# Bringing x in transposed by DMA instead of transposing it on TensorE

## The chip, the cores and the metric

The kernel runs on one core of a Trainium2 chip. The metric is the device time of one execution in microseconds. A core has TensorE (PE in the profile, with weight loads as PEld), VectorE (DVE), ScalarE (ACT), GpSimd (POOL) and SyncE (SP); SP, ACT and POOL also have queues that issue DMAs.

## The reference

One input x of 2048 rows and 448 channels goes through two branches that a gate mixes: attention with 16 query heads of 28 channels over one shared key and value head, and a state-space convolution along the rows.

```python
x = A_x                                              # (1, 2048, 448) bf16
g = _sigmoid((x * gate_w).sum(-1, keepdims=True))
q = (x @ wq).reshape(B, S, H, Dh) ...                # H = 16, Dh = 28
k = x @ wk;  v = x @ wv
scores = einsum("bhqd,bkd->bhqk", q, k) * (Dh ** -0.5)
a = (softmax(scores) @ v) ... @ wo
P = exp(dt * (A_re + 1j*A_im) * l)                   # 448 channels, 256 modes, l = 0..2047
K = einsum("dn,dnl,dn->dl", Cc, P, dB).real          # a kernel of 2048 taps for each channel
b = causal_convolution(K, x) + x * Dskip             # the reference does it by FFT
return g * a + (1 - g) * b
```

## The kernel before, in words

The kernel is written as a list of operations with their data dependences (`Prog.op`, `Prog.dma`). A planner (`Prog.schedule`) gives each operation an estimated duration, a priority `pr` and, where `pg.after[i] = d` is set, a predecessor it has to follow in the plan without waiting for it on the chip; it writes down one fixed order for each engine. `Prog.emit` then puts a semaphore wait where an operation depends on another engine or a DMA. Every DMA is issued on line 140 by the queue that `eng` names, so one line stands for all of them in the profile, and they are told apart by their tiles. An instruction that waits holds back everything behind it on its engine or queue.

**Start.** The K, V and q projections contract over channels, so x is needed with channels on partitions. `loads` brings x in as it lies (four chunks `x0` to `x3` of 512 rows into the tile `tab`), and `prep_x` transposes each chunk: 16 transposing matmuls (L613) into PSUM and two copies to SBUF, on ACT (L623) or DVE (L625). A transposed chunk holds four blocks `T` of 112 channels in 512 columns each, where block T takes channels 4p + T. Chunk 0 lies in `xT`, chunk 1 in a free part of `T`, chunks 2 and 3 in slots of `expT` that are not yet used. The weights are brought in the same channel order (`wks` in `seedw`, `wst` in `mbf`) and spread by DVE copies into `Wk` (L526), `Wq` (L528) and `Wv` (L530, L532).

For each chunk, four matmuls make K (L633), ACT copies it to `kT` (L645), DVE takes the largest absolute value of each row (L640), and 16 small matmuls make V and the gate's argument (L656). When all four chunks are through, DVE takes the largest of the four values (`kap`, L665) and makes `Wb` from it (L667). `qproj` makes q for a group of four heads over 512 rows: four matmuls with `Wq` (L810), a reduction on DVE (L816), one matmul with `Wb` (L819) that adds a bound on each score as one more channel, and a cast to `qT` (L822). So no score can be made before all of K.

**Scores.** 1024 tiles of 128 keys by 512 queries, in sets of two or three: the scores on PE (L1186, or L1209 from a spread copy `qM` of q), one exponential on ACT for the whole set (L1230), and the sums with V on PE (L1248). q is made two groups ahead. A chunk of queries serves four groups; then its successor is brought into `xT`. Chunks 1 to 3 were stored for this in a DRAM scratch `XS` (three stores from SP during the start), and `qproj` reloads them on POOL's queue.

**Convolution.** In the same time `prep_params` transposes six raw parameter arrays on PE (`raw0` to `raw5`, L738) and multiplies them out on DVE (L749); `masters` and `tables` build powers of the modes on DVE (L867 to L937), `kgen` makes the taps on PE, POOL stores them to a DRAM scratch `KP`, SP brings them back as banded tiles (`tload`, into `T` and later `U`), and `conv` multiplies these with a shifted copy `U` of x. `U` is zeroed by one DMA, and x comes once more into `O` by sixteen DMAs, from which POOL copies it into `U` and `T`. These DMAs are planned behind the scratch stores of the transposed x (`self.late`).

Of the kernel before, what the change touches and what calls it, by code (L numbers as in the profile page):

```python
# [12 lines left out]
P = 128  # L13
# [66 lines left out]
class Prog:  # L80
# [55 lines left out]
    def dma(self, pairs, desc, slot, rd=(), wr=(), pr=0, eng="sp", slow=False, extra=0):  # L136
        kw = dict(allow_slow_non_contiguous=True) if slow else {}
# [243 lines left out]
class Kernel:  # L381
# [26 lines left out]
    def alloc(self):  # L408
# [44 lines left out]
        self.XS = nc.dram_tensor("XS_scratch", (3 * DT * XQ,), BF).ap()  # L453
# [40 lines left out]
    def loads(self):  # L494
        pg, ins = self.pg, self.ins
        self.xst = self.tab
        x = ins["A_x"]

        def lx(q):
            pg.dma([(self.xst.v(0, P, q * 4 * D, [[1, 4 * D]]), dram(x, q * 4 * P * D, [[4 * D, P], [1, 4 * D]]))],  # L500
                   (128, 3584), f"x{q}", wr=[("xst", q)])
# [5 lines left out]
        def lraw(k):  # L507
            pg.dma([(raw.v(0, DT, k * 1024, [[1, 1024]]), dram(ins[names[k]], 0, [[1024, DT], [1, 1024]]))],
                   (112, 2048), f"raw{k}", wr=[("raw", k)])
# [3 lines left out]
        lx(0)  # L513
        pg.dma([(wks.v(0, DT, 0, [[1, 112]]), dram(ins["A_wk"], 0, [[112, DT], [1, 112]])),
                (wks.v(0, DT, 112, [[1, 112]]), dram(ins["A_wv"], 0, [[112, DT], [1, 112]])),
                (wks.v(0, DT, 224, [[1, 4]]), dram(ins["gate_w"], 0, [[4, DT], [1, 4]]))],
               (336, 200), "wk", wr=["wks"], eng="act")
        lx(1)
        pg.dma([(wst.v(0, DT, 0, [[1, 4 * D]]), dram(ins["A_wq"], 0, [[4 * D, DT], [1, 4 * D]]))],
               (112, 3584), "wq", wr=["wqs"], eng="act")  # L520
        pg.dma([(self.dtb.v(0, P, 0, [[1, D]]), dram(ins["B_log_dt"], 0, [[0, P], [1, D]]))], (128, 896), "ldt", wr=["dt"], eng="act")
        lraw(0)
        lx(2)
        lx(3)
        lraw(1)
        pg.op("dve", lambda e: e.tensor_copy(self.Wk.v(0, DT, 0, [[32, 16], [1, DH]]),  # L526
                                             wks.v(0, DT, 0, [[DH, 4], [0, 4], [1, DH]])), 300, rd=["wks"], wr=["Wk"])
        pg.op("dve", lambda e: e.tensor_copy(self.Wq.v(0, DT, 0, [[32, 64], [1, DH]]),  # L528
# [71 lines left out]

    def prep_x(self):
        pg = self.pg
        xst, kT = self.xst, self.kT
        sm = self.small
        for q in range(4):
            for hp in range(2):
# [733 lines left out]
```

## Time and profile before

| | |
|---|---|
| median of 3 runs | 516.68 us (514.37 to 519.31) |
| the profiled execution | 515.85 us, span 514.0 us |
| busy: ACT / DVE / PE / POOL | 484.5 / 456.7 / 436.6 / 164.1 us |
| exponentials on ACT, L1230 | 465.8 us in 410 instructions |
| first exponential | at 24.0 us |
| DMA queue of SP and that of ACT | 80.76 MB and 0.57 MB |

The span is that of the profiled execution, from its first to its last instruction; the time has what lies around it too. Busy shares are averages over the span; which engine sets the pace is read for each stage.

### The profile page before, as it was taken

The page shows a single profiled execution, that of the slowest core. Times are in us where ns is not written, and L with a number is a line of the kernel's source. Part 1 is how long each engine was busy: PE and PEld are TensorE (multiplying, and loading weights), DVE is VectorE, ACT ScalarE, POOL GpSimd, SP SyncE. Part 2 cuts the span into 40 slices and gives each one's busy share as a digit, 9 for nine tenths or more (in the row PEclk, how much of TensorE's full clock was granted, in tenths as well). Part 3 has the DMA queues.
Part 4 walks back from the last instruction along what each step waited for, and adds up shares of the span by engine and source line. Part 5 has one row for each costly group of instructions (what it writes and reads, how often), then busy time and mean ns, then how long its engine had stood idle before and what let it go on. Part 6 is the DMA issues. An engine that isn't in the chain of part 4 may idle for free.

```text
span 514.0 us, 16906 instructions
## 1 busy us (share of the span) xinstructions
PE 436.6 (85%) x7376; PEld 199.3 (39%) x7468; DVE 456.7 (89%) x856; ACT 484.5 (94%) x434; POOL 164.1 (32%) x306
## 2 busy tenths in 40 slices
PE   5777968789898999889787889989888889989887
PEld 4532113244442434344343433444333444445542
DVE  3899999999999999999999999999999999972223
ACT  3898899999999999999999999999999999999992
POOL 5103624215123425034305242612313162324110
PEclk9969588999997999999999999999999999999997
DMA  8996189945709484985946767794953766097911
GB/s 256 258 246 166 12 174 110 301 119 153 240 8 279 131 261 59 255 192 157 238 112 192 159 199 179 188 269 117 287 125 117 256 200 215 13 321 227 297 31 36
DMA packets 151603, 91.93 MB, mean 179 GB/s; under 512 B 83469, under 2 KB 147518, under 8 KB 151530
## 3 DMA queue, kind: packets, MB, share of 16 engines
q1 hardware_dynamic: 141978, 80.76, 58.6%
q0 software_dynamic: 8896, 9.53, 7.4%
q8 instruction: 58, 0.95, 0.8%
q10 hardware_dynamic: 656, 0.57, 0.4%
q14 instruction: 15, 0.12, 0.1%
HBM read 73.71 MB, written 5.23 MB: 154 GB/s over the span
## 4 chain that ended last, share of the span: by engine, by line
ACT 77%; PE 11%; DVE 6%; DMA 4%; issue 1%; SPq 1%; ACTq 0%; DVEq 0%; another core or an unknown queue 0%
ACT expT L1230 77%; DMA T<-KP_scratch 3%; PE psS L1209 2%; PE psS L1186 1%; PE psB L1248 1%; DMA seedw<-in_gate_w_dram 1%; PE psX L1020 1%; PE psS L1130 1%; SPq L140 1%; DVE tab L749 1%; PE psS L633 1%; PE psS L810 1%; PE psS L613 0%; PE psS L1020 0%; PE psX L810 0%
## 5 line engine op out<-in xcount | busy, mean ns | idle before, releaser
L1230 ACT ACTIVATE expT<-psS 128x1536 bf16<-128x1536 f32 (+1 forms) x410 | 465.8, 1370 | 9.3 <-PE psS L1186 3.7
L901 DVE TENSOR_TENSOR tab<-tab,mbf 128x512 bf16<-128x512 bf16 (+4 forms) x140 | 139.8, 1001 | 0.0
L1209 PE MATMUL psS<-qM,kT 128*128 128x512 bf16 x301 | 101.8, 399 | 26.9 <-ACT expT L1230 14.2
L1186 PE MATMUL psS<-qT,kT 29*128 29x512 bf16 x570 | 77.4, 398 | 27.0 <-ACT expT L1230 25.1
L1248 PE MATMUL psB<-expT,vaug 128*32 128x512 bf16 x960 | 98.5, 402 | 0.2
L140 POOL DMA_DIRECT2D KP_scratch<-kstg x112 | 61.4, 555 | 109.4 <-DVE kstg L970 96.7
L916 DVE TENSOR_TENSOR tab<-tab 128x256 bf16<-128x256 bf16 (+4 forms) x140 | 77.4, 576 | 0.0
L140 POOL DMA_DIRECT2D qM<-qT x64 | 32.5, 516 | 75.0 <-DVE qT L822 63.0
L1248 PEld LDWEIGHTS psB<-expT,vaug 128*32 128x32 bf16 x960 | 24.6, 93 | 76.4 <-issue 73.4
L140 POOL DMA_DIRECT2D rdenB<-R_scratch x60 | 30.1, 509 | 50.6 <-DMA R_scratch<-denT 50.6
L1186 PEld LDWEIGHTS psS<-qT,kT 29*128 29x128 bf16 x570 | 18.7, 91 | 67.9 <-ACT expT L1230 58.4
L1209 PEld LDWEIGHTS psS<-qM,kT 128*128 128x128 bf16 x390 | 23.9, 99 | 47.6 <-ACT expT L1230 33.9
L1020 PE MATMUL psS<-T,U 128*26 128x128 bf16 (+3 forms) x1728 | 38.9, 221 | 1.3 <-issue 1.0
L1020 PE MATMUL psX<-T,U 128*26 128x128 bf16 (+3 forms) x1536 | 35.4, 223 | 2.2 <-DMA T<-KP_scratch 2.2
L1020 PEld LDWEIGHTS psS<-T,U 128*26 128x26 bf16 (+3 forms) x1728 | 29.9, 105 | 16.0 <-issue 11.6
L1020 PEld LDWEIGHTS psX<-T,U 128*26 128x26 bf16 (+3 forms) x1536 | 27.1, 106 | 15.9 <-issue 9.1
L930 DVE TENSOR_TENSOR tab<-tab,tmp 128x1984 bf16<-128x1984 bf16 x28 | 32.2, 1184 | 0.1
L924 DVE TENSOR_TENSOR tmp<-tmp,mq 128x64 bf16<-128x64 bf16 (+4 forms) x70 | 26.4, 378 | 0.3
L140 POOL DMA_DIRECT2D R_scratch<-denT x15 | 8.9, 591 | 51.5 <-DVE denT L1081 34.4
L847 DVE TENSOR_TENSOR msq<-seedz 128x512 f32<-128x512 f32 (+1 forms) x40 | 24.7, 617 | 0.0
L960 PE MATMUL psS<-tab 128*64 128x128 bf16 x512 | 22.8, 226 | 0.3 <-DVE O L1048 0.2
L140 POOL DMA_DIRECT2D denT<-acc x15 | 11.2, 746 | 32.3 <-DVE acc L1075 32.2
(167 smaller groups left out, 474.4 us busy)
## 6 DMA issues: line engine op xcount, KB each, us to landing
T<-KP_scratch SPq DMA_DIRECT2D x204, 272.0 KB
U<-KP_scratch SPq DMA_DIRECT2D x20, 272.0 KB, 5.6
rdenB<-R_scratch POOLq DMA_DIRECT2D x60, 64.0 KB
U<-cst SPq DMA_DIRECT2D x1, 3584.0 KB, 18.7
qM<-qT POOLq DMA_DIRECT2D x64, 32.0 KB
tab<-in_A_x_dram SPq DMA_DIRECT2D x4, 448.0 KB, 6.4
O<-in_A_x_dram SPq DMA_DIRECT2D x16, 112.0 KB, 2.9
O<-cst SPq DMA_DIRECT2D x1, 1792.0 KB, 9.9
```

Of the source, the lines that this page charges most:

```text
L140: return [e.dma_start(o, i, **kw) for o, i in pairs]
L847: pg.op("dve", lambda e: e.tensor_tensor(m2(msq), z2, z2, ALU.mult), el(2 * n), rd=[kr, ki] + first, wr=["msq"], pr=pr)
L901: mul = lambda e, o, a, b: e.tensor_tensor(o, a, b, ALU.mult)
L916: vo(lambda e, dv=dv, tv=tv, k=k: e.tensor_tensor(dv, dv, tv, ALU.add if k else ALU.subtract), n, [kt[k], kd[k]], [kd[k]])
L924: vo(lambda e, w=w, lv=lv: e.tensor_tensor(rho.v(0, P, (32 - 2 * w) * 2, [[64, 32], [2, w], [1, 2]]), rho.v(0, P, (32 - w) * 2, [[64, 32], ...
L930: vo(lambda e, k=k: e.tensor_tensor(tab.v(0, P, FM + k * FP + 2, [[64, 32], [2, 31], [1, 2]]), tab.v(0, P, lm + k * PL + 62, [[64, 32], [- ...
L960: r = e.matmul(G.v(64 * u, 64, 128 * k, [[1, 128]]), tab.v(0, P, lo + comp * PL + cg * 64 + u, [[2, 64]]), tab.v(0, P, fo, [[64, 2], [mo - ...
L1020: r = e.matmul(ps.v(32 * j, 32 - m0, 128 * k, [[1, 128]]), self.U.v(0, P, (4 * gi + j) % UA // 2 * 128 + 2 * (2 * m0 + par) + j % 2, [[4, ...
L1186: r = e.matmul(self.psS.v(0, P, 512 * b, [[1, 512]]), kT.v(32 * h, DH + 1, 128 * kt, [[1, 128]]), qT.v(32 * h, DH + 1, 512 * (i % 2), [[1, ...
L1209: return e.matmul(self.psS.v(0, P, 512 * b, [[1, 512]]), kT.v(0, P, 128 * kt, [[1, 128]]), self.qM.v(0, P, (i % 2) * XQ + 512 * h, [[1, 51 ...
L1230: pg.op("act", lambda e: e.activation(expT.v(0, P, 512 * es[0], spread(es, n)), self.psS.v(0, P, 512 * bs[0], spread(bs, n)), AF.Exp, scal ...
L1248: r = e.matmul(self.psB.v(32 * h, 32, 0, [[1, 512]]), vaug.v(0, P, 32 * kt, [[1, 32]]), expT.v(0, P, 512 * ring[t], [[1, 512]]), start=(kt ...
```

## The change

x is loaded four times 512 rows with a transposing DMA, straight to where the transposed chunk lay. A block is now 128 contiguous channels: blocks 0 to 2 are channels 0 to 383, and block 3 is channels 320 to 447, whose first 64 partitions repeat channels of block 2. There the weight rows are zero: two memsets on DVE clear `wks` and `wst` first, and the weight loads leave these rows out. Each chunk takes two DMAs, one of three blocks and one of the fourth. The weights come in with rows of 28 channels (wk, wv), 448 (wq) and 1 (gate_w), two DMAs each. The transposes, their copies and the scratch stores are gone, and `qproj` reloads a chunk by the same transposing DMA on SP, where it had been a plain load on POOL.

The order of the first loads on SP becomes: x0, Dskip, x1, x2, x3, raw1 to raw5, zeros of U, O, zeros of Wo, padding. On ACT it becomes: wk, wv, gate_w, log_dt, raw0, wq; all wait for the memsets. On PE the order before the first score becomes: K and V of chunk 0, transposes of raw0, q projection 0, K and V of chunks 1 to 3, the matmul with `Wb`. The transposes of raw1 and the multiplication behind them are planned after the first group's `Wb` matmul and cast, and the copy of V to `vaug` after `Wb`.

```diff
-        xst loads: pg.dma([(self.xst.v(0, P, q * 4 * D, [[1, 4 * D]]), dram(x, q * 4 * P * D, [[4 * D, P], [1, 4 * D]]))],
-               (128, 3584), f"x{q}", wr=[("xst", q)])
+    def xload(self, q, src=None, pr=0):
+        t, o = self.xq(q)
+        src = q if src is None else src
+        x = self.ins["A_x"]
+        pairs = [(t.v(0, P, o + 512 * T, [[512, n], [1, 512]]), dram(x, src * 512 * D + c, [[D, 512], [1, P * n]]))
+                 for T, n, c in ((0, 3, 0), (3, 1, D - P))]
+        return self.pg.dma(pairs, (1536, 256), f"x{q}", wr=self.xk(q), pr=pr, turn=True)   # turn: transpose=True
...
+        pg.op("dve", lambda e: e.memset(wks.v(0, 64, 0, [[1, 228]]), 0.0), 130, wr=["wkz"], pr=-1)
+        pg.op("dve", lambda e: e.memset(wst.v(0, 64, 3 * D, [[1, D]]), 0.0), 180, wr=["wkz"], pr=-1)
+        xo = self.xload(0)
+        two = ((0, P, 0, 3), (64, 64, 3, 1))
+        for k, (w, n) in enumerate(zip(W, (DH, DH, 1))):
+            pg.dma([... for p0, m, T, nT in two], (448, 2 * n), f"wk{k}", rd=["wkz"], wr=[("wks", k)], pr=-6, eng="act", slow=n == 1)
+        lraw(0, "act", -5, ["wkz"])
+        pg.dma([... for p0, m, T, nT in two], (448, 896), "wq", rd=["wkz"], wr=["wqs"], pr=-4, eng="act")
+        pg.dma([... log_dt ...], (128, 896), "ldt", rd=["wkz"], wr=["dt"], pr=-5.5, eng="act")
+        ai = [pg.slots[k] for k in ("raw0", "raw0", "wq")]
+        for q in range(1, 4):
+            xo = self.xload(q)
+            pg.after[xo.i] = ai[q - 1]
+        self.xlast = xo.i
+        # raw1 to raw5, zW, pad, zU, u0, u1: pg.after[...] = self.xlast
...
     def prep_x(self):
-        # transposes (L613) and their copies (L623, L625)
-        # the stores to XS
...
-        self.Wk.v(0, DT, T * P, [[1, P]]), xT.v(0, DT, xo + T * 512, [[1, 512]])
+        self.Wk.v(0, P, T * P, [[1, P]]), xT.v(0, P, xo + T * 512, [[1, 512]])       # likewise Wv, Wq
+        pg.after[va.i] = wb.i
...
     def prep_params(self):
         p1, k1 = trans(1, 1)
+        pg.after[pg.lastw[k1]] = self.first[0]       # the Wb matmul of q group 0
         vt(tt(0), p1, dtb, ALU.mult, [k1, "dt"], [K(0)], 1, unlock=p1)
+        pg.after[pg.lastw[K(0)]] = self.first[1]     # its cast to qT
...
     def qproj(self, i):
         if i in (3, 7, 11):
-            pg.dma([(self.xT.v(0, DT, 0, [[1, XQ]]), dram(self.XS, qc * DT * XQ, [[XQ, DT], [1, XQ]]))],
-                   (112, 4096), "xl", rd=[("XS", qc + 1)], wr=self.xk(0), pr=1, eng="pool", extra=9000)
+            self.xload(0, qc + 1, 1)
```

## The prediction

> **What bounds the kernel now.** I read the page's engines and slices first, then the stages, then the order of time in the first 25 us, then the transfers.
>
> ```profile
> PE 436.6 (85%) x7376; PEld 199.3 (39%) x7468; DVE 456.7 (89%) x856; ACT 484.5 (94%) x434; POOL 164.1 (32%) x306
> ACT  3898899999999999999999999999999999999992
> ```
> ```profile
> 0.00:24.00 24.00, 15.72 (x161) 11.96 (x162) 14.56 (x31) 13.92 (x17) 7.09 (x22) 1.00 0.92 258
> 24.00:64.00 40.00, 32.48 (x184) 10.31 (x186) 38.03 (x88) 36.18 (x34) 15.39 (x24) 0.70 0.62 146
> 64.00:504.00 440.00, 382.21 (x7004) 174.45 (x7091) 400.14 (x731) 434.36 (x384) 141.62 (x261) 0.98 0.68 181
> 504.00:514.00 10.00, 6.15 (x31) 2.59 (x29) 3.99 (x8) 0.00 (x0) 0.00 (x0) 0.82 0.14 46
> ```
> Columns of the stages: start and end, length, busy time of PE, PEld, DVE, ACT, POOL, granted clock, DMA share, GB/s. ScalarE is the bound: between 24 and 504 us it works 470.5 of 480 us, 465.8 of them in the exponentials of L1230, none of which the change touches. The span is a start of 24.0 us, 480 us of exponentials with 9.5 us of holes, and a tail of 10 us. The change can move the start, and the holes.
>
> ```profile
> 10.37 0.63 DVE L528 COPY Wq<-mbf 112x1792 bf16<-112x1792 bf16 x1 [1.70 <-DMA mbf<-in_A_wq_dram]
> ...
> 17.79 1.02 PE L633 MATMUL psS<-expT 112*128 112x512 bf16 x4
> ...
> 19.53 1.04 PE L633 MATMUL psX<-expT 112*128 112x512 bf16 x4 [0.42 <-ACT expT L623]
> ...
> 21.17 0.68 DVE L640 TENSOR_REDUCE small<-psX 128x1 f32<-128x512 f32 x1
> ...
> 22.81 0.69 DVE L822 CAST qT<-psS 128x512 bf16<-128x512 f32 x1 [0.48 <-remote]
> ...
> 24.00 2.37 ACT L1230 ACTIVATE expT<-psS 128x1536 bf16<-128x1536 f32 x2
> ```
> This is the start's last stretch. The first exponential needs the largest key of all 2048 rows (kap), so the fourth K projection, at 19.53, must be done; from its start to the first exponential 4.47 us pass (reduce, kap, Wb, one matmul, a cast, the first scores). That projection waited for ScalarE's copy of the last transposed chunk, not for memory. Without transposes and copies it waits for the transfer itself.
>
> ```profile
> tab<-in_A_x_dram SPq DMA_DIRECT2D x4, 448.0 KB, 6.4
> mbf<-in_A_wq_dram ACTq DMA_DIRECT2D x1, 392.0 KB, 8.1
> U<-cst SPq DMA_DIRECT2D x1, 3584.0 KB, 18.7
> U<-T SPq DMA_DIRECT2D x7, 128.0 KB, 6.3
> KP_scratch<-kstg POOLq DMA_DIRECT2D x112, 16.0 KB, 2.0
> ```
> The last figure of each is the median time from issue to landing. These price the new loads.
>
> **What is removed.** 64 transposes on PE (L613, median 305 ns, pipelined to 7.5 us in four bursts), five copies on ACT (L623, 1.02 us each, 5.1 us) and three on DVE (L625, 1.21 us, 3.6 us), three stores to scratch (1.34 MB). All lie before the first exponential, so their worth is not the sum of their times but how much earlier the fourth projection can run. The matmuls stay as many: the four blocks are now 128 channels deep instead of 112, and each cost 0.38 us for 512 columns either way (the scores have 29 or 128 rows and take 398 and 399 ns).
>
> **The new x loads.** Each chunk is 512 rows by four blocks of 128 channels (the last overlaps the third by 64 channels under zero weights): 512 KB in 2048 pieces of 256 bytes. No transposing load is in the trace, so I bound one. From below, by bytes: the busiest 2 us of the start moved 347 GB/s, 1.5 us a chunk. From above, by pieces: 8192 pieces of 448 bytes (U from cst) landed in 18.7 us, less the 2.0 us that even 16 KB needs: 2.04 ns a piece; with nothing taken off for the landing it is 2.28 ns, 4.7 us a chunk. Pieces of 64 bytes (the U from T group, 5120 in flight together) cost (6.3 − 2.0)/5120 = 0.84 ns. 256 bytes lies halfway between 64 and 448, so I take 1.44 ns, 2.9 us a chunk, bounds 1.5 and 4.7.
>
> The Trainium skill's page "DMA: Bandwidth & Descriptors", section "Latency and other measured facts", gives 261 GB/s for a transposing load with strided rows, which as an estimate makes 2.0 us a chunk; no run here shows it yet, and path A below would then give 18.1 us instead of 21.7.
>
> **Path A, the fourth chunk.** SP issues at 0.8; 2.0 us to the first landing; four chunks at c; the ACT queue's loads share the engines (wq 392 KB, raw0 224, log_dt 112, wk and wv 49, together 0.8 MB at 258 GB/s: about 2.8 us); then 4.5 us to the first exponential. Start = 10.1 + 4c: 21.7 us at 2.9, 16.1 at 1.5, 28.9 at 4.7.
>
> **Path B, Wq.** The order of first loads puts wq last on the ACT queue: the first issue waits for two memsets on DVE (about 1.4 us), and ten issues at 0.45 us end at 5.9 where wq was out by 2.7 before. The memsets cost nothing but this wait. Landing took 8.1 us beside 3 MB of other loads, 5.0 for raw0; I take 6: 11.9. PE's order is fixed: first chunk's K and V, raw0's transposes, then q projection 0, which waits for Wq, and behind it chunks 2 to 4. Wq copy 0.63 and q projection 1.28 give 13.9; three K projections of 1.03 with their V parts (0.5 each) and one wait for ACT's kT copy (0.67) put the fourth's start at 17.1, and 4.5 later is 21.6. On ACT, the sine, the table load of 1.28 and kT(2) stand in the same order and end by about 19.5, a second ahead of need or so. If wq lands two us earlier or later, B moves with it: 19.6 to 23.6.
>
> Both paths give the same: the start ends at 21.7 instead of 24.0, **−2.3 us**.
>
> **What follows.** raw1 to raw5 now stand behind the fourth chunk on SP; 1.1 MB at 258 GB/s is 4.3 us, so they land while the 4.5 us after the fourth projection pass, and PE needs them one by one between the first scores. If that cover is gone, each costs up to 0.9 us of hole. The zeroing of U and the sixteen loads into O come earlier, since 1.34 MB of stores is gone; these feed VectorE's tables, which are done by 480 us with 20 us in hand, so they gain nothing. The holes from 24 to 64 us (3.8 us on ACT) fall while PE's clock is granted at 0.70; I take them as they are, ±1.5.
>
> **The three reloads.** They go from POOL (7.2 us to landing, nobody waited) to SP, two instructions each, between T loads. Such a reload waits for PE's last use of xT, and the T loads behind it wait too; the longest such wait on POOL was 3.9 us. T loads are issued well ahead of the convolutions, and ScalarE lost 1.0 us even where one was awaited for 8.7 us (at 218 us). I count 0, with up to +1 us each.
>
> **Sum.** Span 514.0 − 2.3 = 511.7; the profiled execution's own time lay 1.85 us above its span: 513.6. The median shown is 516.68, 0.8 above that execution, so 514.4. The three runs shown spread over 1.0%, so a difference under 1% is about what a measurement can't tell from no change.
>
> **Rivals.**
> 1. Transposing is slower than plain pieces. Then path A decides as soon as 10.1 + 4c passes 21.6, and the kernel gets slower from c = 3.5 on (10.1 + 4c = 24). For it: no row here has a transposing load, and all four stand in one queue that everything waits for. Against it: no neighbouring row needs more than 4.7. At c = 6 the start ends at 34.1, time 526.8; at 4.8 it is 1% slower. The extreme of it is blocks that go one at a time, 64 of them at 2.0 us, the row for 16 KB: 128 us, time about 631. For that extreme, the Trainium skill's page "VectorE: DVE Perf Modes", section "The three transpose paths", has 1309 ns for a 128x128 block by DMA against 390 on TensorE (the trace: 305 ns); strung together, as an estimate, 84 us and a time of about 587. No run here shows it; the loads in the trace overlap, so this extreme has 0.02 out of this rival's chance.
> 2. The start gains much more: c near 2, wq landing at 10, and fewer holes because PE has less to do before. Start 18.5, holes −1: 510.2. For it: 258 GB/s for the whole start already. Against it: ScalarE's fixed order with the table load, and wq as last of ten issues.
> 3. SP blocks: reloads or prep on SP come late, T loads after them, PE stands in order before the scores, and ScalarE starves. Three places at 2 to 3 us against the gain of 2.3: 520.5. For it: SP already waits 118 us in all for KP writes. Against it: the 1.0 us lost at the longest T wait.
>
> **How the numbers follow.** Forecast 0.45, rival 1 0.23, rival 2 0.22, rival 3 0.10. The forecast's own range is 511.0 to 518.5 (paths A and B by their bounds near the middle, holes ±1.5, run to run ±1.5). Over all cases: down to 508 for rival 2 and up to 527 for rival 1 at c = 6; what lies beyond 527 I put at 0.13, below 508 at 0.06. Faster by over 1% (under 511.5) takes most of rival 2 and a little of the forecast: 0.27. Slower by over 1% (over 521.8) takes nearly all of rival 1 and some of rival 3: 0.28. The rest, 0.45, lies within 1%.
>
> **What would show it.** First exponential at 21 to 22.5 us; the fourth chunk landing at 15 to 18 us and Wq's copy at about 12; no hole over 1.5 us in ScalarE from 64 us on; the tail still 10 us. Wrong if the first exponential starts after 25 us (then see the landing of the x chunks: rival 1), before 19.5 (rival 2), or if the holes after 24 us grow by more than 3 us (rival 3).

## Result

The changed kernel takes 521.06 us (median of 20 runs, 517.78 to 526.85), the kernel before 516.73 us in the same comparison (20 runs). The ratio is 1.0085, 95% interval 1.0062 to 1.0108: slower by 0.85%, where 514.4 us, faster by 0.4%, was forecast. The profiled execution of it took 521.19 us, its span is 519.4 us.

The page of the changed kernel, engines and ScalarE's slices:

```profile
PE 445.4 (86%) x7404; PEld 193.0 (37%) x7404; DVE 454.1 (87%) x855; ACT 480.4 (93%) x429; POOL 161.7 (31%) x303
ACT  3498989999998999998999999999999999999793
```

The stages (columns as before: start and end, length, busy time of PE, PEld, DVE, ACT, POOL, granted clock, DMA share, GB/s):

```profile
0.00:24.00 24.00, 10.66 (x93) 5.35 (x93) 10.73 (x29) 9.17 (x12) 6.96 (x21) 1.00 0.97 198
24.00:64.00 40.00, 31.59 (x196) 9.57 (x195) 38.88 (x88) 36.53 (x36) 14.61 (x24) 0.83 0.69 161
64.00:504.00 440.00, 393.54 (x7038) 174.22 (x7038) 400.45 (x732) 428.36 (x379) 140.17 (x258) 0.97 0.69 180
504.00:519.40 15.40, 9.59 (x78) 3.89 (x78) 3.99 (x8) 6.39 (x7) 0.00 (x0) 0.87 0.10 31
```

ScalarE still sets the pace. The removed work is gone: PE is busy for 10.66 us of the first 24 where it was 15.72, DVE 10.73 instead of 14.56, ACT 9.17 instead of 13.92. Yet the DMA engines are as full as before (share 0.97) and move less: 198 GB/s instead of 258. The start in order of time (start, length, engine, line, operation; in brackets the idle time before it and what ended it):

```profile
0.82 2.70 SPq L140 DMA_TRANSPOSE xT<-in_A_x_dram  x2
...
4.09 2.79 SPq L140 DMA_TRANSPOSE T<-in_A_x_dram  x2
...
6.92 8.59 SPq L140 DMA_TRANSPOSE expT<-in_A_x_dram  x4
...
7.30 1.86 PE L618 MATMUL psS<-xT,expT 128*128 128x512 bf16 x4 [7.30 <-DMA xT<-in_A_x_dram]
...
14.01 0.63 DVE L529 COPY Wq<-mbf 128x1792 bf16<-128x1792 bf16 x1 [0.39 <-DMA mbf<-in_A_wq_dram]
...
14.69 1.89 PE L801 MATMUL psS<-xT,Wq 128*128 128x512 bf16 x4 [2.21 <-DVE Wq L529]
...
16.37 1.91 PE L618 MATMUL psS<-T,expT 128*128 128x512 bf16 x4
...
19.07 1.65 PE L618 MATMUL psS<-expT 128*128 128x512 bf16 x4 [0.25 <-ACT kT L630]
...
19.96 1.28 ACT L750 ACT_TABLE_LOAD   x1
...
20.86 1.02 PE L618 MATMUL psX<-expT 128*128 128x512 bf16 x4
...
21.36 0.67 ACT L630 ACTIVATE kT<-psS,small 128x512 bf16<-128x512 f32 x1
...
22.06 0.69 DVE L625 TENSOR_REDUCE small<-kT 128x1 f32<-128x512 bf16 x1 [2.33 <-ACT kT L630]
...
25.50 1.45 ACT L1222 ACTIVATE expT<-psS 128x1536 bf16<-128x1536 f32 x1 [0.92 <-PE psS L1178]
```

The first three lines are the issues of the x loads on SP. Behind the first K projection comes what path B of the prediction consists of: Wq copied, q projection 0, second, third and fourth K projection (they follow one another on PE without a wait for memory), and the first exponential at 25.50 instead of 24.00. The lines of ACT at 19.96 and 21.36 and of DVE at 22.06 belong to a third path, which the prediction had ahead of need: ScalarE loads a table and copies the third chunk's keys, and the reduction behind it waited for that copy, which ended at 22.03, as late as the fourth K projection (21.88).

The span splits so, from the timeline of ScalarE:

| | before | after | difference |
|---|---|---|---|
| first exponential starts | 24.0 | 25.5 | +1.5 |
| from there to the end of the last one | 479.7 | 484.9 | +5.2 |
| of that, ScalarE idle (holes) | 9.0 | 13.4 | +4.4 |
| tail | 10.3 | 9.0 | −1.3 |
| span | 514.0 | 519.4 | +5.4 |

So two things are to be explained: a start that comes later although work was taken out of it, and holes in a stretch of which the change touches little. The pair of profiles differs by 5.4 us, the medians by 4.3: a single profile can be off by about a us.

### The profile page after: what moved, and what is told of

The parts are those of the page before. It is cut to its first block, busy times and chain, and to the rows that moved or that the text cites. A ratio compares the mean times of both kernels' runs of the same rounds, so it can differ in the third digit from the quotient of the medians.

```text
span 519.4 us, 16871 instructions
## 1 busy us (share of the span) xinstructions
PE 445.4 (86%) x7404; PEld 193.0 (37%) x7404; DVE 454.1 (87%) x855; ACT 480.4 (93%) x429; POOL 161.7 (31%) x303
## 4 chain that ended last, share of the span: by engine, by line
ACT 45%; DVE 34%; PE 11%; DMA 5%; SPq 1%; issue 1%; ACTq 1%; DVEq 0%
ACT expT L1222 45%; DVE tab L893 10%; DVE tab L908 5%; DMA T<-KP_scratch 4%; DVE tab L922 2%; PE psS L1178 2%; DVE tmp L916 2%; PE psS L1201 1%; SPq L140 1%; DVE kstg L962 1%; PE psB L1240 1%; DMA mbf<-in_A_wq_dram 1%; DVE msq L839 1%; PE psX L1012 1%; DVE mbf L859 1%
## 5 line engine op out<-in xcount | busy, mean ns | idle before, releaser
L1222 ACT ACTIVATE expT<-psS 128x1536 bf16<-128x1536 f32 (+1 forms) x410 | 466.7, 1346 | 14.8 <-PE psS L1178 6.5
L1201 PE MATMUL psS<-qM,kT 128*128 128x512 bf16 x390 | 122.6, 399 | 12.2 <-ACT expT L1222 11.6
L1012 PE MATMUL psX<-T,U 128*32 128x128 bf16 x1984 | 45.7, 224 | 3.1 <-issue 2.6
L1012 PEld LDWEIGHTS psX<-T,U 128*32 128x32 bf16 x1984 | 35.6, 106 | 20.4 <-issue 14.5
L1201 PEld LDWEIGHTS psS<-qM,kT 128*128 128x128 bf16 x390 | 24.1, 98 | 47.4 <-ACT expT L1222 33.9
L1012 PE MATMUL psS<-T,U 128*26 128x128 bf16 (+3 forms) x1280 | 31.3, 224 | 3.8 <-DMA T<-KP_scratch 3.4
L1012 PEld LDWEIGHTS psS<-T,U 128*26 128x26 bf16 (+3 forms) x1280 | 23.7, 106 | 16.6 <-issue 8.8
L952 PE MATMUL psS<-tab 128*64 128x128 bf16 x576 | 25.4, 224 | 0.0
```

Of the source, the lines that this page charges most:

```text
L952: r = e.matmul(G.v(64 * u, 64, 128 * k, [[1, 128]]), tab.v(0, P, lo + comp * PL + cg * 64 + u, [[2, 64]]), tab.v(0, P, fo, [[64, 2], [mo - ...
L1012: r = e.matmul(ps.v(32 * j, 32 - m0, 128 * k, [[1, 128]]), self.U.v(0, P, (4 * gi + j) % UA // 2 * 128 + 2 * (2 * m0 + par) + j % 2, [[4, ...
L1201: return e.matmul(self.psS.v(0, P, 512 * b, [[1, 512]]), kT.v(0, P, 128 * kt, [[1, 128]]), self.qM.v(0, P, (i % 2) * XQ + 512 * h, [[1, 51 ...
L1222: pg.op("act", lambda e: e.activation(expT.v(0, P, 512 * es[0], spread(es, n)), self.psS.v(0, P, 512 * bs[0], spread(bs, n)), AF.Exp, scal ...
```

## Experiments

Theories. **S**, the start: path B is longer than forecast, because Wq comes late among full DMA engines and because PE computes slowly. **R**, the reloads on SP: T loads stand behind them and come late (rival 3 of the prediction). **P**, the planner: it laid out the work for a start that the chip doesn't keep. **O**, the order: any new order of this kernel has other holes, whatever caused it.

All kernels in one table. The ratio is to the kernel before in the same comparison, and each group of runs has a comparison of its own, so ratios are to be compared and not times; the other columns are from the one profiled execution. "First exp" is the start of the first exponential, "phase" the time from there to the end of the last one, "holes" ScalarE's idle time in it. "PE for T" is the time that PE waited for T loads, from the list of waits.

| kernel | time, us | ratio (95%) | first exp | phase | holes | PE for T |
|---|---|---|---|---|---|---|
| before | 516.73 | | 24.0 | 479.7 | 9.0 | 2.4 |
| after | 521.06 | 1.0085 (1.0062–1.0108) | 25.5 | 484.9 | 13.4 | 3.8 |
| e1 weights first | 522.23 | 1.0109 (1.0072–1.0147) | 28.1 | 485.3 | 13.6 | 3.3 |
| e2 no reloads | 519.99 | 1.0068 (1.0035–1.0102) | 24.3 | 486.8 | 15.3 | 0 |
| e3 after, replanned | 524.67 | 1.0156 (1.0116–1.0197) | 25.9 | 491.4 | 19.5 | 6.3 |
| e4 before, replanned | 517.80 | 1.0031 (0.9995–1.0066) | 24.0 | 480.6 | 8.9 | 0.6 |
| e5 after, true costs | 526.11 | 1.0201 (1.0134–1.0269) | 23.7 | 487.5 | 15.1 | 5.6 |
| e6 before, false costs | 521.68 | 1.0076 (1.0038–1.0115) | 23.4 | 489.7 | 17.7 | 3.4 |
| e7 plain loads | 523.61 | 1.0137 (1.0095–1.0179) | 29.6 | 484.0 | 12.4 | 0.4 |
| e8 wq behind x0 | 522.42 | 1.0110 (1.0049–1.0171) | 26.1 | 487.4 | 15.7 | 2.4 |
| e9 after, order of before | 522.68 | 1.0106 (1.0059–1.0152) | 25.1 | 487.7 | 15.1 | 5.2 |
| e10 before, order of after | 536.09 | 1.0356 (1.0293–1.0419) | 30.8 | 493.1 | 20.6 | 0.9 |
| e11 before, replanned | 519.02 | 1.0041 (1.0002–1.0080) | 24.0 | 483.2 | 11.6 | 2.5 |
| e12 before, replanned | 517.30 | 0.9974 (0.9936–1.0012) | 24.3 | 485.2 | 13.2 | 0 |
| e13 e9 without reloads | 518.48 | 1.0025 (1.0000–1.0050) | 24.0 | 484.6 | 12.8 | 0.3 |
| e14 set order undone | 525.48 | 1.0162 (1.0117–1.0207) | 25.2 | 486.9 | 11.3 | 6.0 |
| e15 PE kept busy | 520.72 | 1.0047 (1.0015–1.0078) | 25.1 | 487.4 | 15.4 | 4.3 |
| e16 e9, reloads behind | 523.73 | 1.0142 (1.0100–1.0184) | 24.4 | 490.2 | 18.4 | 5.4 |
| e17 e16, PE kept busy | 521.92 | 1.0103 (1.0057–1.0149) | 24.1 | 487.4 | 15.3 | 1.0 |
| e18 after, reloads behind | 524.37 | 1.0184 (1.0133–1.0235) | 25.7 | 488.4 | 16.7 | 3.4 |

### The start: e1, e7, e8, e14, e15

**e1**: only the order of ACT's first transfers is changed, to wk, wq, raw0, log_dt, wv, gate.

```diff
+            rank = {"wk0": 0, "wq": 1, "raw0": 2, "ldt": 3, "wk1": 4, "wk2": 5}
+            first = sorted((i for i in od if ops[i].slot in rank), key=lambda i: rank[ops[i].slot])
+            self.pg.order["act"] = first + [i for i in od if ops[i].slot not in rank]
```

> The changed kernel with only ACT's first DMAs in another order: wk, wq, raw0, log_dt, wv, gate_w, so that wq is issued third instead of ninth. Every other engine keeps its order. If the late Wq sets the start (it was copied at 14.0 us), the copy comes at about 10.5 us and the first exponential moves from 25.5 to between 22.5 and 23.5 us (the fourth chunk's landing at 17 to 18 us then takes over), and the time falls by the same 2 to 3 us, ratio 1.003 to 1.005. If the start is worth nothing because VectorE's chain of tables sets the pace behind it, the first exponential moves and the ratio stays near 1.0085.

It missed, in the wrong direction. wq was issued at 2.53 instead of 6.36 us and still copied later:

```profile
16.58 0.62 DVE L533 COPY Wq<-mbf 128x1792 bf16<-128x1792 bf16 x1
```

The DMA engines were full (a share of 0.98 over the first 24 us). wq landed 6.4 us after its issues, by 9.6, but with it in front the first x chunk came two us later (the first K projection ran at 9.44 instead of 7.30), and wv and gate, which DVE copies ahead of Wq, came last (13.50 and 13.95). DVE's fixed order then had its work on log_dt and raw0 before the copy of Wq too. So it was the order on DVE, and not the landing of wq, that made the copy late here. The start moved by 2.6 us, and the median by 1.2.

**e7**: the same tiles from plain loads of as many bytes. This kernel leaves the transposing out, so K, V and q are made from x in another arrangement.

```diff
-        pairs = [(t.v(0, P, o + 512 * T, [[512, n], [1, 512]]), dram(x, src * 512 * D + c, [[D, 512], [1, P * n]]))
-                 for T, n, c in ((0, 3, 0), (3, 1, D - P))]
-        return self.pg.dma(pairs, (1536, 256), f"x{q}", wr=self.xk(q), pr=pr, turn=True)
+        pairs = [(t.v(0, P, o + 512 * T, [[1, 512 * n]]), dram(x, src * 512 * D + c, [[4 * D, P], [1, 512 * n]]))
+                 for T, n, c in ((0, 3, 0), (3, 1, 4 * D - 512))]
+        return self.pg.dma(pairs, (1536, 256), f"x{q}", wr=self.xk(q), pr=pr)
```

> The changed kernel with plain loads of the same bytes into the same tiles (x is not transposed, so K, V and q are made from x in another arrangement); orders and queues stay. If the transposing costs engine time of its own (141 to 152 GB/s at a full DMA share in the first 6 us), the plain loads land the first chunk by about 5 us instead of 7.3, Wq is copied at about 10.5 instead of 14.0, and the first exponential comes at 20 to 22 us instead of 25.5; the reloads land in 3 to 4 us instead of 5. If the order and the small weight loads set the start, Wq still comes at 13 to 14 us and the first exponential at 24 to 25.5.

It missed too. The plain loads did move faster: 278 and 294 GB/s in the second and third 2 us, where the transposing ones moved 152 and 141, at a full DMA share in both, and the first two of 384 KB landed in 3.2 and 3.7 us. So SP was free early and issued the zeroing of U, 3.6 MB, at 8.57 us; wq, issued from 6.23 on, then shared the engines with it and took 10.4 to 11.3 us to land instead of 6.4 to 7.0:

```profile
18.14 0.63 DVE L529 COPY Wq<-mbf 128x1792 bf16<-128x1792 bf16 x1 [2.40 <-DMA mbf<-in_A_wq_dram]
```

The start ended at 29.6 us. In this order a faster x load makes the start slower, because Wq is what it waits for.

**e8**: wq moved to SP behind the first chunk, planned with the landings expected of that order (as in e5 below, with other figures).

```diff
-                for p0, m, T, nT in two], (448, 896), "wq", rd=["wkz"], wr=["wqs"], pr=-4, eng="act")
+                for p0, m, T, nT in two], (448, 896), "wq", rd=["wkz"], wr=["wqs"], pr=-4)
...
-        ai = [pg.slots[k] for k in ("raw0", "raw0", "wq")]
+        ai = [pg.slots[k] for k in ("wq", "wq", "wq")]
```

> The kernel of the true costs, with wq issued on SP right behind the first chunk instead of last on ACT's queue. If Wq's late landing sets the start, Wq is copied at 9 to 10.5 us, q projection 0 runs by 11, the fourth chunk's landing (18 to 19 us) becomes the bound, and the first exponential comes at 23 to 24 us; with holes as in the kernel of the true costs the ratio is 0.998 to 1.003. If not, the first exponential stays at 25 to 26 us.

```profile
9.98 0.62 DVE L533 COPY Wq<-mbf 128x1792 bf16<-128x1792 bf16 x1
...
10.66 1.89 PE L805 MATMUL psX<-xT,Wq 128*128 128x512 bf16 x4 [1.98 <-DVE Wq L533]
...
14.28 1.87 PE L622 MATMUL psS<-T,expT 128*128 128x512 bf16 x4 [1.73 <-DMA T<-in_A_x_dram]
...
20.14 0.81 PE L622 MATMUL psS<-expT 128*128 128x512 bf16 x3 [0.85 <-DMA expT<-in_A_x_dram]
```

Wq was there four us earlier, as expected, and now the second and the fourth chunk were waited for: path A took path B's place and the fourth K projection ran at 20.14. From there 6.0 us passed to the first exponential at 26.1, not 4.5: ScalarE's last copy of keys came at 23.89, behind its work on raw0 and a table load, and PE stood waiting for it. What one load gained here the others lost. The ratio, 1.0110, missed the 0.998 to 1.003 expected.

**e14**: the set order undone, to that of before (wk, wv, gate, wq, log_dt on ACT, raw0 on SP between the second and third chunk, no load held back for another; the priorities `pr` of these loads go as well).

```diff
...
-        lraw(0, "act", -5, ["wkz"])
-        ai = [pg.slots[k] for k in ("raw0", "raw0", "wq")]
         for q in range(1, 4):
             xo = self.xload(q)
-            pg.after[xo.i] = ai[q - 1]
+            if q == 1:
+                lraw(0)
```

> The changed kernel with its set order of first loads undone, to that of before: wk, wv, gate, wq, log_dt on ACT's queue, raw0 on SP between the second and third chunk, nothing held back for another. The planner then puts the q projection behind all four K projections, so Wq (path B) is out of the chain and the x chunks alone (path A) set the start. If the start was late for Wq (theory S): four chunks at 3.6 us from 2.8 us on land by 17 to 18, the fourth K projection runs at 18 to 19 and the first exponential at 22.5 to 23.5. If the transposing loads themselves are too slow among the others (rival 1 of the prediction), the fourth chunk is waited for and the first exponential stays at 25 to 27. The rest of the order is a new one, worth half a per cent either way: time 513 to 521.

```profile
14.41 1.17 PE L617 MATMUL psS<-expT 128*128 128x512 bf16 x4 [0.42 <-DMA expT<-in_A_x_dram]
...
16.81 1.04 PE L617 MATMUL psS<-expT 128*128 128x512 bf16 x3 [0.54 <-DMA expT<-in_A_x_dram]
...
19.36 1.04 PE L800 MATMUL psS<-xT,Wq 128*128 128x512 bf16 x4 [0.61 <-ACT kT L629]
...
25.21 1.45 ACT L1221 ACTIVATE expT<-psS 128x1536 bf16<-128x1536 f32 x1 [3.95 <-PE psS L1177]
```

Half of it held: with Wq out of the chain the fourth K projection ran at 16.8 us, straight from its chunk's landing, 4.1 us earlier than in the changed kernel. That it still gave no earlier first exponential was not expected: in the new plan the q projection stands behind the K projections and waits for ScalarE's last kT copy, so its reduction, Wb, cast and scores take the 8.4 us to 25.2. The chunks themselves are not too slow: with path A's own terms 16.8 = 5.6 + 4c gives c = 2.8. The time lay above the 513 to 521 us expected.

**e15**: matmuls on the identity, results unread, 30 before the first K projection and 30 before the q projection.

```diff
+            def dummy(e):
+                for k in range(30):
+                    r = e.matmul(t.v(0, P, o, [[1, P]]), self.ident.v(0, P, 0, [[1, P]]), self.ident.v(0, P, 0, [[1, P]]),
+                                 start=True, stop=True, tile_position=(0, 0))
+                return r
```

> The changed kernel with 30 matmuls of 128 columns on the identity, whose results nobody reads, put on PE before the first K projection and 30 before the q projection, where PE idled. In the changed kernel the first K projection, the q projection and the next two K projections took 1.86, 1.89, 1.91 and 1.65 us, the fourth 1.02. If they were slow because PE had been idle, all now take 1.0 to 1.3 us and the first exponential moves from 25.5 to 23.3 to 24.0; time 519. If something else made them slow (the loads, the clock granted), they stay at 1.65 to 1.9 and the first exponential at 25.4 to 26.

```profile
12.85 3.05 PE L413 MATMUL psS<-ident 128*128 128x128 bf16 x30
...
15.95 0.81 PE L819 MATMUL psS<-xT,Wq 128*128 128x512 bf16 x3
...
16.60 1.03 PE L636 MATMUL psS<-T,expT 128*128 128x512 bf16 x4
...
18.41 1.04 PE L636 MATMUL psS<-expT 128*128 128x512 bf16 x4 [0.29 <-ACT kT L648]
...
20.99 0.67 ACT L648 ACTIVATE kT<-psS,small 128x512 bf16<-128x512 f32 x1
...
25.13 1.45 ACT L1240 ACTIVATE expT<-psS 128x1536 bf16<-128x1536 f32 x1 [0.92 <-PE psS L1196]
```

The mechanism is shown: with PE coming from work, the second and third K projection take 1.03 and 1.04 us where they took 1.91 and 1.65 (the first one, after 3.4 us of dummies and a short gap, still took 1.73). The fourth ran at 19.58 instead of 20.86. Of these 1.3 us only 0.4 reached the first exponential, since ScalarE's copy of the third chunk's keys (20.99 us, behind its work on raw0 and a table load), level with the fourth K projection in the changed kernel, was now last. The time went to 1.0047; the intervals of this and of the changed kernel overlap.

### The plan and the order: e3 to e6, e10 to e12

**e3**, **e4**, **e11** and **e12** change one constant of the planner, so that it picks a new order without any change of the work: `SEM_NS` from 56 to 60 in the kernels after (e3) and before (e4), `PORT` from 0.55 to 0.50 (e11) and DVE's latency from 82 to 92 (e12) in the kernel before.

> The changed kernel with one constant of the planner moved (semaphore delay 60 instead of 56 ns), so that all engines get another order of equal standing, while the program's work is the same. If the loss comes from what the change does (start and reloads), the ratio stays at 1.0085 within 0.003. If the loss is the luck of one order, it can land anywhere from 1.000 to 1.015, and the holes lie in other places.

> The kernel before with the same constant moved. It shows how much a new order alone is worth on that side: within 0.002 of 1 if orders are alike, up to 0.006 off if an order's luck is of the size of the change's effect. Its first exponential should stay at 24 us.

> The kernel before, planned with another share for the port that VectorE and GpSimd have in common (0.50 instead of 0.55): a third order for the same work with the same start. Theory O, if the order shown before was among the better ones: phase 481 to 487 us, ratio 1.001 to 1.010. If orders planned for the true start are alike: phase 480 us, ratio within 0.003 of 1.

> The kernel before, planned with VectorE's latency at 92 instead of 82 ns: a fourth order. Expected as for the third: phase 481 to 487 us and ratio 1.001 to 1.010 if the order before was among the better ones, within 0.003 of 1 otherwise.

The three new orders of before came to 1.0031, 1.0041 and 0.9974, the one of after to 1.0156. In one profile holes ranged from 8.9 to 13.2 us for the same work. An order is worth some half a per cent either way, and the order of the kernel before is not a singular one, as e12 shows.

**e5** tells the planner the starts that the profile showed (each transposing load 3.6 us, the projections 1.9 us, the landings of the first loads); **e6** tells the planner of the kernel before landings that are 2.2 to 4.5 us too early. Of e5's edit:

```diff
+    LATE = {"x0": 1500, "wk0": 1000, "wk1": 1900, "wk2": 2300, "ldt": 3000, "raw0": 3000, "wq": 4000, "x1": -1500, "x2": -1500, "x3": -1500}
+        o.ns = 3600.0 if turn else o.ns
+        if slot not in self.slots:
+            o.extra += self.LATE.get(slot, 0)
```

> The changed kernel, whose planner is told what the trace showed: 3.6 us for a transposed chunk, the weights' landings 1 to 4 us later, 1.9 us for the first K projections. Its due time for the first exponential moves from 20.3 to 25.6 us, where the chip had it at 25.5. Theory P (the extra holes come from orders made for a start 5 us too early, so that engines meet each other out of step): the holes behind the first exponential fall from 13.4 to about 9 us, the first exponential stays at 25 to 26 us, and the ratio falls to between 1.001 and 1.005. Rival (the holes belong to the transposing reloads or to chance): the holes stay at 13 us or more and the ratio at 1.0085 or above.

> The kernel before, whose planner is told landings of the first loads 2 to 4.5 us earlier than they are, so that its due time for the first exponential is 19.3 us instead of 22.8; nothing else is changed. Theory P: the first exponential stays at 24 to 25.5 us, but the holes behind it grow from 9 to 12 us or more, ratio 1.005 to 1.012, without any transposing load. Rival: the holes stay at 9 to 10 us and the ratio within 0.003 of 1.

e6 lost 0.8% with no transposing load in it, as theory P has it, but e5 speaks against P as the cause: planned for the start that the profile showed, and with a first exponential at 23.7 us (25 to 26 was expected), earlier than before, the changed kernel was at 1.0201, worse than with the wrong plan. It is one new order, so this is no proof. What e6 shows can be O as well.

**e10** puts the work of before into the sequence in which the planner picked the work of after; for this the operation that loads the sine's table is tied to another input.

> The reverse: the work of the kernel before (plain loads, transposes, copies, scratch stores, reloads on POOL), picked in the sequence of the changed kernel; the transposes of a chunk stand one chunk ahead of its K projection. Theory O: holes 12 us or more, phase 483 us or more, ratio 1.005 to 1.012 though no load is transposing. Rival W: holes 9 us, phase 480 us, ratio within 0.004 of 1, less or more by the start.

It came to 1.0356, but for a reason of its own: transposes and stores stand late in a sequence that was not made for them, the first exponential came at 30.8 us, and one hole of 10.4 us follows a store to scratch. It tells nothing on the holes of the changed kernel.

### The reloads: e2, e9, e13, e16, e17, e18

**e2**: the changed kernel without the three reloads, order otherwise the same.

```diff
+            gone = [i for i in od if ops[i].slot == "x0"][1:]
+            self.pg.order["sp"] = [i for i in od if i not in gone]
```

> The changed kernel without its three reloads of xT (q of all four chunks is made from chunk 0; nothing else is left out, and every engine keeps its order). If the transposing reloads on SP hold up the T loads behind them and so make holes in ScalarE, the holes after 95, 212 and 330 us shrink and the time falls by 1.5 to 3 us, ratio 1.003 to 1.006. If they cost nothing, the ratio stays within 0.001 of 1.0085.

PE waited for no T load any more, but the holes did not fall and the time hardly (1.0068 against 1.0085, intervals overlapping).

**e9**: the work of after forced into the sequence in which the planner picked the work of before, so that the order is out of the comparison. The reloads stand where they stood, on SP instead of POOL.

> The changed kernel's work (transposing loads, reloads on SP, no transposes, copies or stores), with every operation picked in the very sequence in which the planner of the kernel before picked it; new operations stand where those they replace stood, raw0 stays on ACT's queue. Theory O (the holes belong to the order, not to the change's work): phase of exponentials 480 to 482 us as before, holes 9 to 10 us, and the time differs only by the start; with a first exponential between 22 and 26 us the ratio is 0.996 to 1.005. Rival W (the holes belong to the change's own work: reloads and T loads behind them on SP, other landings): holes 13 us or more, phase 484 us or more, ratio 1.006 or above.

1.0106: the loss is there in the order of before too. Its largest hole, in order of time:

```profile
329.86 3.73 SPq L146 DMA_TRANSPOSE xT<-in_A_x_dram  x2
...
341.93 1.37 PE L1001 MATMUL psS<-T,U 128*32 128x128 bf16 x44 [2.00 <-DMA T<-KP_scratch]
...
343.89 1.45 ACT L1211 ACTIVATE expT<-psS 128x1536 bf16<-128x1536 f32 x1 [2.69 <-PE psS L1167]
```

The reload kept SP for 3.73 us, the T loads behind it were issued later by as much (the first at 333.69), PE waited for one of them with the scores behind it, and ScalarE ran dry. Then PE's clock fell while it caught up, and three more holes followed (windows of the same kernel, columns as above):

```profile
338.00:342.00 4.00, 1.61 (x32) 0.50 (x25) 4.00 (x5) 3.20 (x4) 0.55 (x1) 0.93 0.96 280
342.00:344.00 2.00, 2.00 (x51) 1.25 (x51) 0.14 (x1) 0.11 (x1) 0.00 (x0) 0.50 1.02 325
344.00:346.00 2.00, 1.67 (x29) 0.83 (x30) 1.31 (x3) 1.69 (x2) 0.00 (x0) 0.50 1.08 379
```

**e13**: e9 without the reloads (edit of e2).

> The kernel of e9 (the changed work in the sequence of before) without its three reloads of x: the later q projections read the first chunk's data again. In e9 a hole of 2.7 us at 344 us, with 1.1 us more in the next three, followed a T load that stood on SP behind a reload (issued at 329.9, 3.7 us). If the reloads on SP make such holes, this place goes back to what before shows there (none), the holes fall from 15.1 to about 11 us and the ratio to about 1.003. If those holes are chance (the granted clock fell to 0.50 in just these 6 us), holes of that size stay somewhere, 13 to 16 us in all, and the ratio stays at 1.008 to 1.011.

As theory R had it: 518.48 us, 1.0025 (1.0000 to 1.0050), 4.2 us below e9 where the interval of e9 begins at 1.0059. PE waited 0.3 us for T loads instead of 5.2, and the hole of 2.69 us at 344 us shrank to 0.79 (at 342). The holes as a whole fell less than expected, from 15.1 to 12.8 us. About 1 us of the 4.2 may be the start, which was 24.0 here and 25.1 in e9 with the same instructions in it.

**e16**: e9 with the second and third reload moved on SP behind the T loads that they stood in front of. **e18**: the same in the changed kernel's own order.

```diff
+            for i in [i for i in sp if ops[i].slot == "x0"][2:]:
+                k = sp.index(i)
+                n = k + 1
+                while ops[sp[n]].slot[0] == "T":
+                    n += 1
+                sp.insert(n - 1, sp.pop(k))
```

> The kernel of e9 (all of the changed work in the sequence of before) with the second and third reload moved on SP behind the T loads that they stood in front of (12 and 4 of them); the q projections that read them come 30 us later. If the reloads cost because T loads stand behind them, the time falls to that of e13, which had none: ratio 1.001 to 1.005 against 1.0106 of e9. If e9 was slow for another reason, or the reloads cost by their traffic, it stays at 1.008 to 1.012.

> The changed kernel as it is, with the second and third reload moved on SP behind the 8 and 12 T loads that they stood in front of. If the reloads' place is what its phase of exponentials lost, the holes fall from 13.4 to about 10 us and the ratio from 1.0085 to about 1.003. If in this order the planner had already made room for them (e2, without the reloads, gave 1.0068), the ratio stays at 1.006 to 1.009.

Both missed: 1.0142 and 1.0184. The hole moved with the reload. In e16, at the third one:

```profile
345.88 5.01 SPq L146 DMA_TRANSPOSE xT<-in_A_x_dram  x2
...
365.61 1.05 PE L1008 MATMUL psX<-T,U 128*32 128x128 bf16 x32 [2.28 <-DMA T<-KP_scratch]
...
367.66 1.02 ACT L1218 ACTIVATE expT<-psS 128x1024 bf16<-128x1024 f32 x1 [2.52 <-PE psS L1197]
```

and in e18 one of 3.03 us at 363.5. SP has T loads and shuffles in a row from 326 to 372 us; whichever comes behind the reload is late by the 3.7 to 5.0 us for which it keeps the queue. So no place tried between the T loads was free of cost; the records show SP held by the reload and the loads behind it issued late. What part its bytes on the DMA engines have in that is not told apart here.

**e17**: e16 with PE kept busy as in e15 (30 and 24 matmuls).

> The kernel of e16 with PE kept busy in the start: 30 matmuls on the identity before the first K projection, 24 before the q projection, results unread. In e9 the q projection and the second K projection took 1.89 and 1.78 us; with a PE that comes from work they take 1.0, ScalarE's kT copies are not held by its table load in this sequence, and the first exponential comes at 23.0 to 24.0, 0.5 to 1.5 us earlier than in e16. Ratio 0.998 to 1.003. If an earlier start only brings PE's slow clock forward, the ratio is that of e16.

```profile
12.84 0.63 DVE L543 COPY Wq<-mbf 128x1792 bf16<-128x1792 bf16 x1 [3.35 <-DMA mbf<-in_A_wq_dram]
...
13.53 1.04 PE L815 MATMUL psS<-xT,Wq 128*128 128x512 bf16 x4 [1.45 <-DVE Wq L543]
...
14.60 1.02 PE L632 MATMUL psS<-T,expT 128*128 128x512 bf16 x4
...
18.82 1.02 PE L632 MATMUL psX<-expT 128*128 128x512 bf16 x4 [1.08 <-DMA expT<-in_A_x_dram]
...
24.09 1.45 ACT L1236 ACTIVATE expT<-psS 128x1536 bf16<-128x1536 f32 x1 [0.40 <-PE psS L1192]
```

With fast projections the fourth K projection waits for its chunk, which landed at 18.8 us: path A binds now, with c = (18.8 − 5.6)/4 = 3.3, and the first exponential comes at 24.1, where the kernel before has it with all its transposes. The ratio, 1.0103, missed what was expected: 4.4 us of holes stood at 495 to 503 us, where PE's clock was granted at 0.50. No complete version of the changed kernel that was run beat the kernel before.

## Why the prediction was wrong, by its steps

By spans, 511.7 was forecast and 519.4 came: 7.7 us off. 3.8 of them are the start (−2.3 forecast, +1.5 measured), 5.2 the phase of exponentials (0 forecast), and the tail gave back 1.3. That 521.06 still lies in the range given, 508 to 527, is owed to the width that rivals 1 and 3 gave it and not to this sum.

**The start, path B: the step that failed.** The path was the right one; its terms were mis-sized, by 3.9 us together (25.5 instead of 21.6): 2.1 for Wq's copy, 1.6 for PE, 0.2 behind the fourth K projection.

Wq's copy came at 14.0 instead of 11.9. Its landing was about right: 6 us after the last issue were forecast, 6.3 came. The issuing was not: ten issues on ACT's queue were priced at 0.45 us each, to end at 5.9, and they ran from 1.47 to 7.69, 0.62 each. What made them longer is open; the transposing is not needed for it, since in e7, with plain x loads, they took 0.59 each. In e2, whose start has the same instructions, the copy came at 12.8, so more than a us varies between executions.

On PE, from the copy's end to the fourth K projection 6.2 us passed instead of 4.6. The terms q projection 1.28 and K projection 1.03 were read from the last two rows of this view of the kernel before, in which PE had worked almost without a gap since 8.72 us (first K and V, 16 transposes, raw0); the first row, behind a gap of 1.3 us, was not heeded.

```profile
8.72 1.89 PE L633 MATMUL psS<-xT,expT 112*128 112x512 bf16 x4 [1.32 <-DVE xT L625]
...
12.16 1.28 PE L810 MATMUL psS<-xT,Wq 112*128 112x512 bf16 x4
...
14.33 1.03 PE L633 MATMUL psS<-T,expT 112*128 112x512 bf16 x4
```

In the changed kernel PE has nothing to do while Wq is late, and starts slowly after it. e15 and e17 show that work put in that gap, here plain matmuls, brings 1.03 back; how much of that the removed transposes did by themselves was not tried. The Trainium skill's page "TensorE: Matmul & The Clock Gate", section "Part 1: The HAM clock gate (the "warmup" mystery)", has the rule that the prediction left out: an array that has idled works at half its clock until some 3.4 us of activity have passed. The trace agrees on the factor: 1.86 to 1.91 us from idle, 1.02 to 1.04 after work. On the time it gives no single figure: 3.8 us of work were enough in e15 (raw0's transposes and dummies from 12.13 to 15.9), while the third K projection of the changed kernel, 4.4 us after PE had resumed, still took 1.65.

The prediction's remark that ScalarE's third copy of keys would end by 19.5, ahead of need, failed too: it ended at 22.03. So two paths end together, and e15, which hastened one of them, gained 0.4 us.

Two sums do not come out of their own terms: 0.8 MB at 258 GB/s are 3.1 us and not 2.8, and two K projections with their V parts and the wait put the fourth's start at 17.5 and not 17.1. Either makes its path 22.0 us, which is still earlier than 24.0.

**The bound behind it, path A.** By path A's other terms a chunk costs 2.8 (e14) to 3.3 us (e17); 2.9 was forecast, and the bounds 1.5 to 4.7 hold. Rival 1, slow transposing loads from c = 3.5 on, is near but did not decide: in the changed kernel PE waited for no chunk after the first. Its test, a first exponential after 25 us, came out as the prediction had worded it, and would have named the wrong cause. From the Trainium skill's page "DMA: Bandwidth & Descriptors", section "Latency and other measured facts", 2.0 us a chunk was worked out; the trace does not agree: between 2 and 6 us, when little but x was loaded and the engines were full, 141 to 152 GB/s were moved instead of 261. That transposing is slower than plain loads of the same bytes, as rival 1 has it, e7 shows with 278 and 294 GB/s in the same stretch; but a faster load alone did not help there.

**What held.** From the fourth K projection to the first exponential 4.47 us were forecast, 4.64 came (20.86 to 25.50). The exponentials' own time stayed (466.7 us of L1222 against 465.8 of L1230), the tail was 9.0 for 10.

**The holes: "I take them as they are, ±1.5".** They grew by 4.4 us, rival 3's sign. Rival 3 is shown to act in the order of before (e9 against e13). It fits that in the eleven kernels with transposing reloads in SP's queue PE waits 1.0 to 6.3 us for T loads, 4.2 on the mean, and in the eight without reloads there 0 to 3.4, 1.3 on the mean (e7, with plain reloads on SP, 0.4). The term "0, with up to +1 us each" was mis-sized: three reloads cost up to 4.2 us there, of which a us may be the start. The reading that misled was the 118 us for which SP waits for KP writes: a queue that waits much on the whole still has stretches, 326 to 372 us here, with nothing to spare.

**What stays open.** In the changed kernel's own order taking the reloads away gained only 0.2% (e2), less than the measurement resolves. Of its 4.4 us of holes 0.6 lie before 90 us, 0.8 at 160 to 170, 1.0 between 220 and 400, and 2.0 after 480. The largest hole there, 1.57 us before 486.95, follows 1.81 us in which PE stood still and the profile names no releaser; then PE's clock fell:

```profile
488.00:492.00 4.00, 4.00 (x98) 2.60 (x101) 0.59 (x2) 3.09 (x4) 1.11 (x3) 0.58 0.16 43
```

The kernel before had 1.00 there and ScalarE worked through these 4 us. How much of the rest belongs to the order (worth −0.3 to +0.8% in e4, e6, e11 and e12), to the reloads and to the clock, these runs do not separate. The order alone does not make the loss: the four orders of the old work planned for its own start lie at 0.997 to 1.004, the eleven complete kernels of the changed work at 1.005 to 1.020.

VectorE as a second pace setter was not tested. It works 99% of the time from 64 to 450 us in both kernels, and its last table is done at 460.2 us instead of 458.8, late by about as much as the start. The chain that ended last runs 34% through it, 6% before; but with the old work in another order (e11) it is 28%, so this does not single the change out.

Reloads by another queue than SP's were not tried. The Trainium skill's page "DMA: Bandwidth & Descriptors", section "DMA Transpose (X-bar)", names SP and ACT as issuers of the plain transposing load and gives GpSimd a gather with transpose instead, which no run here shows. ACT is the engine that sets the pace.

## What to carry to other kernels

Removing work from PE can leave it idle ahead of the matmuls that the chain needs, and then they are slow: price them from rows in which PE came from idle. In this start, with all DMA engines full, a new order of loads only shared out lateness, so find the load that the chain waits for before speeding up another, and price its issue too. And a transfer moved to a queue is charged for the time it holds that queue, in its tightest stretch and not on its average.

## What the runs showed of the hardware

- A transposing load holds the issuing queue far longer than a plain one: a pair (384 and 128 KB) took SP 2.7 to 2.8 us for the first two chunks of the changed kernel, 4.3 us each for the next two, and 2.8 to 6.0 us in the later reloads of all kernels. A plain pair of the same bytes took 0.8 to 1.4 us (e7). A transposing load of x landed in 5.1 us at the median.
- With the DMA engines full, transposing loads moved 141 to 152 GB/s between 2 and 6 us, plain ones of the same bytes 278 to 294 (e7).
- PE out of idle ran four matmuls of 512 columns in 1.86 to 1.91 us, and in 1.02 to 1.04 after some 3 us (e14, from 11.37 to 14.41) to 6 us of work (the changed kernel, from 14.69 to 20.86), while the profile's granted clock read 1.00 for slow and fast ones alike in the changed kernel. In the start the granted clock row does not show this state.
- The granted clock fell to 0.50 for some us when PE caught up after a wait in e9 (342 to 348 us, behind a wait of 2.0 us, with 3.8 us of holes on ScalarE in all), e16 (366 to 368) and e18 (364 to 366). It does not always: in the changed kernel PE worked 1.20 of the 3 us from 238 to 241, and the clock stayed at 1.00 behind it.
- The same first instructions gave a first exponential between 24.3 and 25.7 us (e2, after, e18): the copy of Wq came between 12.8 and 14.2 us in these three executions.
